# Reordering the start of an attention-plus-FFN kernel: loads, turns and sums of the first attention, pacing of batch 1, place of the late weight pieces

## The chip, the cores and the metric

One core of a Trainium2 chip. The metric is the device time of one execution in microseconds (us). Most executions of a program agree within a few tenths of a per cent; here they scatter by about 1%. The engines are called PE (TensorE, matmuls), DVE (VectorE), ACT (ScalarE), POOL (GpSimd) and SP (SyncE, which only issues DMAs here).

## The reference

```python
# q, k, v: (8 batches, 12 heads, 448 tokens, 64), float32
scores = scale * q @ k^T
m = max(scores); e = exp(scores - m)
attn = e / (sum(e) + exp(-m) + 1e-9) @ v           # softmax with one more term in the sum
x = attn, heads side by side                       # (3584 tokens, 768)
xn = x / sqrt(mean(x*x) + 1e-6) * rms_g
out = (silu(xn @ w_gate) * (xn @ w_val)) @ w_out    # 768 -> 1536 -> 768
```

## The kernel before

The program is one long PE stream. Batch 0's attention runs first ("first attention"). Then the FFN runs batch by batch and, between its matmul groups, the attention of the batches after it. A table of `(nominal time, operation)` says where each piece of attention work goes into the FFN's stream; the nominal times only fix an order. The matmul groups used as landmarks below are "gate m" and "value m", six matmuls each, for column block m of `w_gate` and `w_val`.

Heads go in pairs, and pairs in groups of two, three groups to a batch. For groups 0 to 6, PE transposes q and k ("turns" them, `emit_T`). From group 7 on a DMA does that (`turn_qk`, issued by SP), after POOL has cast q and k to bf16:

```python
    def cast_qkv(n, i, eng):
        ...
        eng.tensor_copy(out=dst, in_=staged[n, i].rearrange("p h c d -> p c h d"))

    def turn_qk(n):
        for i, src in enumerate((qk_bf[n, 0], qk_bf[n, 1])):
            nc.sync.dma_start_transpose(
                out=turned(n)[:, i, 0:LQ].rearrange("p (b t) -> p b t", t=P),
                in_=src.rearrange("p c h d -> p (c h d)"))
```

POOL issues the early loads too, and it works in program order. This is the part of batch 1's table that decides POOL's order (NG is 3, so `2 * NG + 1` is group 7 and `2 * NG + 2` is group 8):

```python
    for t, f in ((2.4, lambda: cast_qkv(NG, 2, G)), (3.5, lambda: loads(NG + 2)),
                 (3.6, lambda: cast_qkv(NG + 1, 2, G)), (3.7, lambda: load_w(4)),
                 (7.3, lambda: loads(2 * NG)), (7.4, lambda: cast_qkv(NG + 2, 2, G)),
                 (10.5, lambda: loads(2 * NG + 1)), (19.5, lambda: cast_qkv(2 * NG, 2, G)),
                 (19.6, lambda: casts(2 * NG + 1)), (19.7, lambda: loads(2 * NG + 2)),
                 (23.0, lambda: turn_qk(2 * NG + 1)), (26.0, lambda: casts(2 * NG + 2)),
                 (29.0, lambda: turn_qk(2 * NG + 2))):
        ops.append((t, f))
    for i in range(KF // 4):
        ops.append((22.0 + 0.01 * i, lambda i=i: load_w_o(i)))      # w_out, 3 x 768 KB
```

`warm(n)` issues n matmuls on zeros whose results nobody reads; they keep PE busy where it would idle:

```python
    def warm(n):
        ps = ps_f.tile([128, 512], FP32, name="warm_ps", tag="f")
        for _ in range(n):
            nc.tensor.matmul(ps, lhsT=blank[:, 0:128], rhs=blank, start=True, stop=True)
```

The softmax here doesn't subtract the row's maximum and nothing guards it: scores larger than these inputs give would overflow.

## Time and profile before

| | before |
|---|---|
| median of 3 runs | 485.04 us (484.3 to 485.96) |
| span of the profiled execution | 483.3 us |
| first FFN matmul | 39.4 us |
| PE busy | 95% of the span |

From the page of the kernel before, the busy time by engine, and then two rows of the 40 slices (12 us each). A digit is the busy share in tenths, and PEclk is the granted TensorE clock in tenths of full speed:

```profile
PE 460.6 (95%) x4053; PEld 247.9 (51%) x4056; DVE 242.0 (50%) x625; ACT 250.6 (52%) x363; POOL 98.4 (20%) x119
...
PE   8978988899989999999999999999999999999996
...
PEclk9999899999999999999999999999999999999998
```

PE fills nearly everything after the eighth slice. What is open lies in the first 90 us, and there PEclk has one dip, at about 50 us.

The window table of the kernel before: a stretch, its length, each engine's busy time, the mean granted clock, the DMA engines' share and GB/s.

```profile
36.00:48.00 12.00, 9.91 (x92) 5.08 (x93) 7.26 (x15) 6.12 (x9) 3.21 (x5) 1.00 0.16 41
48.00:60.00 12.00, 10.47 (x123) 5.49 (x123) 5.33 (x12) 8.55 (x12) 6.93 (x10) 0.86 1.16 213
60.00:76.00 16.00, 13.79 (x195) 7.99 (x192) 10.97 (x32) 11.88 (x16) 2.50 (x4) 1.00 0.95 191
76.00:88.00 12.00, 9.29 (x96) 5.26 (x96) 11.51 (x30) 3.92 (x9) 5.54 (x6) 1.00 0.07 13
88.00:105.00 17.00, 16.90 (x142) 8.48 (x138) 8.80 (x20) 10.00 (x14) 9.68 (x12) 1.00 1.05 236
105.00:120.00 15.00, 15.00 (x138) 7.75 (x138) 7.62 (x18) 9.39 (x13) 1.04 (x1) 1.00 1.21 180
```

PE has holes up to 88 us and none after. A clock of 0.86 in 48 to 60 us is 3.4 us at half speed.

The timeline of ACT in the kernel before, the first attention (start, duration, instruction, and in brackets the idle time before it and who ended it):

```profile
18.80 3.53 ACT L210 ACTIVATE p_sb_108<-s_ps 112x896 bf16<-112x896 f32 x4 [0.74 <-PE s_ps L205]
...
27.09 1.82 ACT L210 ACTIVATE p_sb_114<-s_ps 112x896 bf16<-112x896 f32 x2 [1.07 <-PE s_ps L205]
```

ACT, which has the most to do there, stands idle for scores that wait for a turn. That is what the first part of the change is aimed at.

### The profile page before, as it was taken

To read this page: it belongs to the slowest core of one execution; us is meant where nothing else is said; L and a number is where in the kernel's file an instruction comes from. 1 tells how busy PE (TensorE), PEld (TensorE's weight loads), DVE (VectorE), ACT (ScalarE), POOL (GpSimd) and SP (SyncE) were. 2 spreads that over 40 slices of the span, in tenths; PEclk is the share of its full clock that TensorE was granted. 3 is DMA by queue.
4 is the path that set the end of the run, shared out by engine and by line. 5 is a ranking of instruction groups with operands and counts; after the bars stand their busy time and mean duration, and the time that the engine had idled before them with its cause. 6 is when DMAs were issued, how large, how long until landed. Compare 5 with 4: busy or idle time off the path is not lost.

```text
span 483.3 us, 9859 instructions
## 1 busy us (share of the span) xinstructions
PE 460.6 (95%) x4053; PEld 247.9 (51%) x4056; DVE 242.0 (50%) x625; ACT 250.6 (52%) x363; POOL 98.4 (20%) x119
## 2 busy tenths in 40 slices
PE   8978988899989999999999999999999999999996
PEld 3544444455545555455455555554455555555563
DVE  4585469655634145855643136665653147655200
ACT  4975774555555665454556555554555562222221
POOL 6432511740403022313003012304001001000000
PEclk9999899999999999999999999999999999999998
DMA  8991990799919989289009979279104320200133
GB/s 121 205 222 35 217 229 16 182 227 181 219 40 230 182 207 200 62 198 182 1 20 229 182 181 212 51 151 210 27 2 114 96 80 3 55 1 1 34 98 99
DMA packets 86841, 60.48 MB, mean 125 GB/s; under 512 B 50710, under 2 KB 81756, under 8 KB 86796
## 3 DMA queue, kind: packets, MB, share of 16 engines
q1 hardware_dynamic: 73820, 43.60, 42.2%
q0 software_dynamic: 12976, 16.26, 18.0%
q8 instruction: 32, 0.52, 0.4%
q14 instruction: 13, 0.11, 0.1%
HBM read 47.19 MB, written 11.01 MB: 120 GB/s over the span
## 4 chain that ended last, share of the span: by engine, by line
PE 80%; issue 8%; DVE 6%; POOL 3%; ACT 2%; POOLq 0%; DVEq 0%
PE o_ps L335 23%; PE v_ps L310 19%; PE g_ps L310 15%; PE u_ps L235 8%; PE s_ps L205 8%; PE s_ps L310 5%; DVE xsq L261 2%; PE warm_ps L354 2%; DVE x_sb L239 1%; DVE ht_sb L321 1%; POOL v_sb_120 L154 1%; ACT t_sb L314 1%; PE qkt_ps L178 1%; ACT wg_bf L119 1%; DVE pair_t_102 L181 0%
## 5 line engine op out<-in xcount | busy, mean ns | idle before, releaser
L310 PE MATMUL v_ps<-xnt_sb,wv_bf 128*128 128x448 bf16 x576 | 126.3, 355 | 3.4 <-DVE ht_sb L321 3.1
L335 PE MATMUL o_ps<-wo_bf,ht_sb 128*128 128x384 bf16 x672 | 116.5, 326 | 0.0
L310 PE MATMUL g_ps<-xnt_sb,wg_bf 128*128 128x448 bf16 x444 | 96.3, 353 | 1.1 <-DVE xnt_sb L280 0.7
L335 PEld LDWEIGHTS <-ht_sb 128*128 128x128 bf16 x672 | 62.6, 98 | 46.2 <-issue 7.8
L310 PEld LDWEIGHTS <-wv_bf 128*128 128x128 bf16 x576 | 53.0, 98 | 56.2 <-issue 12.3
L310 PEld LDWEIGHTS <-wg_bf 128*128 128x128 bf16 x576 | 52.5, 98 | 54.5 <-issue 11.2
L314 ACT ACTIVATE t_sb<-g_ps 128x448 f32<-128x448 f32 x74 | 40.2, 543 | 73.3 <-PE g_ps L310 73.1
L210 ACT ACTIVATE p_sb_108<-s_ps 112x896 bf16<-112x896 f32 x64 | 55.8, 915 | 17.1 <-PE s_ps L205 17.1
L210 ACT ACTIVATE p_sb_114<-s_ps 112x896 bf16<-112x896 f32 x64 | 56.3, 915 | 12.5 <-PE s_ps L205 12.5
L338 ACT ACTIVATE out_sb<-o_ps 128x384 f32<-128x384 f32 x56 | 27.4, 490 | 66.9 <-PE o_ps L335 61.9
L210 ACT ACTIVATE p_sb_111<-s_ps 112x896 bf16<-112x896 f32 x64 | 55.8, 916 | 11.0 <-PE s_ps L205 11.0
L238 DVE RECIPROCAL recip<-u_ps 112x4 f32<-112x4 f32 x96 | 17.0, 177 | 81.9 <-PE u_ps L235 81.8
L293 POOL TENSOR_TENSOR rinv<-ms,neghalf 112x2 f32<-112x2 f32 x16 | 11.1, 716 | 157.3 <-DVE ms L286 149.6
L239 DVE TENSOR_TENSOR x_sb<-u_ps,recip 112x256 bf16<-112x256 f32 x96 | 40.7, 424 | 3.3
L154 POOL CAST q_bf<-q_f 112x1024 bf16<-112x1024 f32 x17 | 18.0, 1059 | 103.4 <-DMA q_f<-in_q_dram 90.1
L205 PE MATMUL s_ps<-qk_t 64*128 64x448 bf16 x272 | 37.5, 354 | 0.0
L261 DVE CUSTOM_DVE_ANT_0 xsq<-x_sb 112x256 bf16<-112x256 bf16 (+3 forms) x64 | 36.0, 563 | 1.7
L314 ACT ACTIVATE t_sb<-s_ps 128x448 f32<-128x448 f32 x22 | 11.9, 543 | 38.5 <-PE s_ps L310 33.3
L310 PE MATMUL s_ps<-xnt_sb,wg_bf 128*128 128x448 bf16 x132 | 28.6, 352 | 0.0
L235 PEld LDWEIGHTS <-p_sb_114 112*128 112x128 bf16 (+1 forms) x512 | 20.0, 98 | 7.7 <-DVE x_sb L239 1.4
L235 PEld LDWEIGHTS <-p_sb_108 112*128 112x128 bf16 (+1 forms) x512 | 19.8, 99 | 7.2 <-issue 2.9
L235 PEld LDWEIGHTS <-p_sb_111 112*128 112x128 bf16 (+1 forms) x512 | 19.7, 97 | 6.7 <-issue 2.1
(274 smaller groups left out, 385.6 us busy)
## 6 DMA issues: line engine op xcount, KB each, us to landing
q_f<-in_q_dram SPq DMA_DIRECT2D x15, 448.0 KB, 4.9
k_f<-in_k_dram SPq DMA_DIRECT2D x15, 448.0 KB, 6.2
v_f<-in_v_dram SPq DMA_DIRECT2D x15, 448.0 KB, 6.9
v_f<-in_v_dram POOLq DMA_DIRECT2D x9, 448.0 KB, 10.5
out_dram<-out_sb SPq DMA_DIRECT2D x8, 336.0 KB, 2.8
wg_bf<-in_moe_w_gate_dram POOLq DMA_DIRECT2D x4, 576.0 KB, 8.1
wv_bf<-in_moe_w_val_dram POOLq DMA_DIRECT2D x4, 576.0 KB, 12.5
wo_bf<-in_moe_w_out_dram POOLq DMA_DIRECT2D x3, 768.0 KB, 20.7
```

The source lines that it names most:

```text
L154: eng.tensor_copy(out=dst, in_=staged[n, i].rearrange("p h c d -> p c h d"))
L205: nc.tensor.matmul(s_ps[:, hh, 0:S], lhsT=k_t[r, k0:k0 + 128], rhs=qs[r], start=True, stop=True)
L210: nc.scalar.activation(out=p_v, in_=s_ps[0:P, :, 0:S], func=AF.Exp, scale=scale)
L235: nc.tensor.matmul(u_ps[:, qc, :], lhsT=p_sb[0:K, q0:q0 + 128], rhs=v_sb[0:K, c, h, :], start=(c == 0), stop=(c == C - 1))
L238: nc.vector.reciprocal(out=recip, in_=u_ps[0:P, :, D:E1])
L239: nc.vector.tensor_tensor(out=x_tiles[b][:, :, h * D:(h + 1) * D], in0=u_ps[0:P, :, 0:D], in1=recip.to_broadcast([P, C, D]), op=ALU.mult)
L261: nc.vector.tensor_tensor_reduce(out=xsq[:, 0:n], in0=x_c, in1=x_c, scale=1.0, scalar=0.0, op0=ALU.mult, op1=ALU.add, accum_out=acc)
L293: nc.gpsimd.tensor_tensor(out=rinv[:, cs], in0=ms[:, cs], in1=neghalf[:, cs], op=ALU.pow)
L310: nc.tensor.matmul(ps[:, 0:S], lhsT=w[:, dk, m * 128:(m + 1) * 128], rhs=xnt_tiles[b][:, :, dk, :], start=(dk == 0), stop=(dk == KD - 1))
L314: nc.scalar.activation(out=t, in_=ps[:, 0:S], func=AF.Tanh, scale=0.5)
L335: nc.tensor.matmul(o_ps[:, 0:HN], lhsT=ht_tiles[b2][:, fk, c * 128:(c + 1) * 128], rhs=wo_bf[:, fk, n * HN:(n + 1) * HN], start=(fk == 0), ...
L338: nc.scalar.activation(out=o_sb[:, n * HN:(n + 1) * HN], in_=o_ps[:, 0:HN], func=AF.Copy, scale=0.5)
```

## The change

The intent: let each pair's weighted sums run one pair behind its scores, place the turns where q and k arrive, move v casts off VectorE, and issue the late pieces of the gate and value weights among the loads of batch 1 so that the DMA engines don't idle from 36 to 46 us. The core of the diff:

```diff
-            if part == len(parts(b)) - 1 and b < NPE and c % 2 == 1:
+            if part > 0 and b < NPE and c % 2 == 1:              # more sums of squares on ACT
...
-        for cs in (slice(0, 2), slice(2, 4)):
-            nc.gpsimd.tensor_tensor(out=rinv[:, cs], in0=ms[:, cs], in1=neghalf[:, cs], op=ALU.pow)
+        nc.gpsimd.tensor_tensor(out=rinv, in0=ms, in1=neghalf, op=ALU.pow)
...
-    for j, t0 in enumerate((4.0, 5.6, 7.2, 8.8, 10.4, 12.0)):
-        ops += [(t0 + 0.39 * i, op) for i, op in enumerate(micro_ops(NP + j))]
+    for j, t0 in enumerate((3.6, 5.6, 7.6, 9.6, 11.6, 13.6)):
+        ops += [(t0 + 0.49 * i, op) for i, op in enumerate(micro_ops(NP + j))]
...
-    for i in range(2 * KD):
-        ops.append((9.0 + 0.45 * i, lambda: scale_w(1, V)))
+    for i in range(KD):
+        ops.append((9.6 + 0.35 * i, lambda: scale_w(1, V)))
+    ops.append((14.65, lambda: scale_w(KD, V)))
...
-    for t, f in ((2.4, lambda: cast_qkv(NG, 2, G)), (3.5, lambda: loads(NG + 2)),
-                 (3.6, lambda: cast_qkv(NG + 1, 2, G)), (3.7, lambda: load_w(4)),
-                 (7.3, lambda: loads(2 * NG)), (7.4, lambda: cast_qkv(NG + 2, 2, G)),
-                 (10.5, lambda: loads(2 * NG + 1)), (19.5, lambda: cast_qkv(2 * NG, 2, G)),
-                 (19.6, lambda: casts(2 * NG + 1)), (19.7, lambda: loads(2 * NG + 2)),
-                 (23.0, lambda: turn_qk(2 * NG + 1)), (26.0, lambda: casts(2 * NG + 2)),
-                 (29.0, lambda: turn_qk(2 * NG + 2))):
+    for t, f in ((2.4, lambda: (cast_qkv(NG, 2, G), load_w(2))),
+                 (4.3, lambda: (loads(NG + 2), cast_qkv(NG + 1, 2, G), load_w(2))),
+                 (8.3, lambda: loads(2 * NG)),
+                 (11.5, lambda: (cast_qkv(NG + 2, 2, G), loads(2 * NG + 1))),
+                 (17.1, lambda: (cast_qkv(2 * NG, 2, G), loads(2 * NG + 2))),
+                 (23.0, lambda: casts(2 * NG + 1)), (25.0, lambda: turn_qk(2 * NG + 1)),
+                 (27.5, lambda: casts(2 * NG + 2)), (29.5, lambda: turn_qk(2 * NG + 2))):
         ops.append((t, f))
     for i in range(KF // 4):
-        ops.append((22.0 + 0.01 * i, lambda i=i: load_w_o(i)))
+        ops.append((20.0 + 0.01 * i, lambda i=i: load_w_o(i)))
...
-    for i in range(2):
-        load_qkv(1, i, G)
     load_qkv(0, 2, G)
     make_identity(nc, ident_f)
+    loads(1)
...
-        (2, 1): [lambda: emit_AV(0, 0)], (2, 2): [lambda: emit_AV(0, 1)],
+        (1, 1): [lambda: emit_AV(0, 0)], (1, 2): [lambda: emit_AV(0, 1)],
+        (1, 3): [lambda: emit_T(2), lambda: load_w(4), lambda: cast_qkv(1, 2, G)],
... (the rest of this table moves in the same way)
```

More of the change, by code (lines that the diff above doesn't have):

```diff
@@ L430 @@
         ffn += [(TB, lambda b2=b2, c=c, n=n: emit_B(b2, c, n)) for c in range(7) for n in range(2)]
-    spans = {2: (20, 55), 3: (55, 88), 4: (88, 134), 5: (134, 171), 6: (171, 213), 7: (213, 250)}
+    spans = {2: (21, 55), 3: (55, 88), 4: (88, 134), 5: (134, 171), 6: (171, 213), 7: (213, 250)}
     ops = []
@@ L437 @@
         ops += [(t0 + (t1 - t0) * i / len(seq), op) for i, op in enumerate(seq)]
-    for j, t0 in enumerate((2.3, 3.4, 5.6, 7.2, 8.8, 10.4, 18.6, 22.0)):
+    for j, t0 in enumerate((2.3, 4.2, 6.2, 8.2, 11.2, 12.2, 19.5, 22.5)):
         ops.append((t0, lambda j=j: emit_T(NP + j)))
-    for j, t0 in enumerate((4.0, 5.6, 7.2, 8.8, 10.4, 12.0)):
-        ops += [(t0 + 0.39 * i, op) for i, op in enumerate(micro_ops(NP + j))]
-    ops.append((14.9, lambda: (emit_stats(1, 1), emit_root(1))))
+    for j, t0 in enumerate((3.6, 5.6, 7.6, 9.6, 11.6, 13.6)):
+        ops += [(t0 + 0.49 * i, op) for i, op in enumerate(micro_ops(NP + j))]
+    ops.append((16.7, lambda: (emit_stats(1, 1), emit_root(1))))
     for c in range(C):
-        ops.append((16.5 + 0.6 * c, lambda c=c: emit_scale(1, c)))
-        ops.append((18.7 + 1.1 * c, lambda c=c: emit_turn_x(1, c)))
-    for i in range(2 * KD):
-        ops.append((9.0 + 0.45 * i, lambda: scale_w(1, V)))
+        ops.append((18.3 + 0.6 * c, lambda c=c: emit_scale(1, c)))
+        ops.append((20.4 + 1.1 * c, lambda c=c: emit_turn_x(1, c)))
+    for i in range(KD):
+        ops.append((9.6 + 0.35 * i, lambda: scale_w(1, V)))
+    ops.append((14.65, lambda: scale_w(KD, V)))
     def loads(n):
@@ L494 @@
     between = {
-        (0, 0): [lambda: emit_T(1), lambda: [load_qkv(2, i, G) for i in range(2)]],
-        (0, 1): [gains, lambda: warm(1)], (0, 2): [lambda: warm(2)], (0, 3): [lambda: warm(2)],
-        (1, 0): [lambda: warm(2)], (1, 1): [lambda: warm(2)],
-        (1, 2): [lambda: emit_T(2), lambda: cast_qkv(0, 2, V)],
-        (1, 3): [lambda: [load_qkv(1, 2, G), load_qkv(2, 2, G), load_w(4)], lambda: warm(2)],
-        (2, 0): [lambda: warm(2)],
-        (2, 1): [lambda: emit_AV(0, 0)], (2, 2): [lambda: emit_AV(0, 1)],
@@ L502 @@
-        (2, 3): [lambda: emit_T(3), lambda: loads(NG)],
-        (3, 0): [lambda: emit_AV(1, 0)], (3, 1): [lambda: emit_AV(1, 1)],
-        (3, 2): [lambda: emit_T(4), lambda: cast_qkv(1, 2, V)],
-        (3, 3): [lambda: warm(2)],
-        (4, 0): [lambda: emit_AV(2, 0), lambda: cast_qkv(2, 2, V)],
-        (4, 1): [lambda: emit_AV(2, 1), lambda: emit_stats(0, 0, (0, 1))],
-        (4, 2): [lambda: emit_T(5), lambda: emit_stats(0, 0, (2, 3)), lambda: loads(NG + 1)],
-        (4, 3): [lambda: emit_AV(3, 0)],
@@ L510 @@
-        (5, 0): [lambda: emit_AV(3, 1)], (5, 1): [lambda: emit_AV(4, 0)],
-        (5, 2): [lambda: emit_AV(4, 1), lambda: emit_stats(0, 1, (0, 1))],
-        (5, 3): [lambda: emit_stats(0, 1, (2, 3))],
+        (0, 0): [lambda: emit_T(1)],
+        (0, 1): [gains, lambda: [load_qkv(2, i, G) for i in range(2)], lambda: warm(1)],
+        (0, 2): [lambda: cast_qkv(0, 2, V), lambda: load_qkv(2, 2, G), lambda: warm(2)],
+        (0, 3): [lambda: warm(2)],
+        (1, 0): [lambda: warm(2)],
+        (1, 1): [lambda: emit_AV(0, 0)], (1, 2): [lambda: emit_AV(0, 1)],
@@ new lines @@
+        (1, 3): [lambda: emit_T(2), lambda: load_w(4), lambda: cast_qkv(1, 2, G)],
+        (2, 0): [lambda: emit_T(3)],
+        (2, 1): [lambda: emit_AV(1, 0)], (2, 2): [lambda: emit_AV(1, 1)],
+        (2, 3): [lambda: loads(NG), lambda: warm(1)],
+        (3, 0): [lambda: warm(1), lambda: cast_qkv(2, 2, G)],
+        (3, 1): [lambda: emit_AV(2, 0)], (3, 2): [lambda: emit_AV(2, 1)],
+        (3, 3): [lambda: emit_T(4), lambda: emit_stats(0, 0, (0, 1))],
+        (4, 0): [lambda: emit_T(5), lambda: emit_stats(0, 0, (2,))],
@@ L513 @@
+        (4, 1): [lambda: emit_AV(3, 0), lambda: emit_stats(0, 0, (3,))],
+        (4, 2): [lambda: emit_AV(3, 1), lambda: loads(NG + 1)],
+        (4, 3): [lambda: warm(1)],
+        (5, 0): [lambda: warm(1)],
+        (5, 1): [lambda: emit_AV(4, 0)], (5, 2): [lambda: emit_AV(4, 1)],
+        (5, 3): [lambda: emit_stats(0, 1)],
     }
@@ L518 @@
                 f()
-    scale_w(3, A)
     emit_AV(NP - 1, 0)
     emit_AV(NP - 1, 1)
+    scale_w(1, A)
     emit_root(0)
-    scale_w(3, V)
+    scale_w(2, V)
+    scale_w(1, A)
     warm(14)
@@ L526 @@
         emit_scale(0, c)
+    scale_w(1, V)
     for c in range(C):
         emit_turn_x(0, c)
+    scale_w(1, V)
     scale_w(3, A)
```

## The prediction

> **What bounds the kernel now.** The page gives TensorE (PE) 95% busy over 483.3 us and 80% of the chain that ended last. By the window table PE is busy 387 of 395 us from 88 us on, which the change hardly touches. What can be won lies before:
>
> 1. First attention, 7.9 to 31.2 us: 24 exponentials on ACT, busy 20.8 of 23.3 us. The timeline shows it idle 0.74 us at 18.8, 0.23 at 23.4, 1.07 at 27.1, 0.41 at 29.3, waiting for scores, which wait for VectorE's copy of turned q/k, behind v casts (0.69 us) and sums of squares (0.56).
> 2. Norm, scale and turn of batch 0, 31.2 to 39.4 us: VectorE first has 4 sums of 0.43 us; the root is two POOL operations (0.91, 0.68).
> 3. First FFN with batch 1's attention, 39.4 to 88 us: PE idles about 7 us. Scores wait for exponentials 3.8 us in seven waits; u waits 1.31 us for VectorE at 78.5; scores wait 1.15 us at 87.9 for a copy queued behind x scales. The granted clock is halved for 3.4 us at 51, costing about 1.7 us; this fits the Trainium skill, "TensorE: Matmul & The Clock Gate", "What's actually happening" (half rate after an idle window of about 3.4 us).
>
> DMA is full from 8 to 36 us, then idle to 46 us: POOL waits 8.8 us for a q buffer before issuing the late weight pieces, which land at 56 to 65 us.
>
> **What the change does.**
> - Sums one pair behind, v loaded earlier, turns spread, two v casts moved to POOL (1.06 us each, off the path): two of six turns still stand directly before their scores, so about 1.4 of 2.45 us ACT idle stays. Gain 1.0 us.
> - Two of four second-part sums go to ACT, one root operation for two: VectorE frees 0.95 us, partly given back by 0.37 us of weight scaling between x scales and turns. Gain 0.4 us.
> - Late weights come before the q loads, landing at 41 to 56 us. Batch 1's pairs are spaced 2.0 units, not 1.6, so ACT has more FFN time per pair: 3.8 us of waits fall to 1.5, gain 2.3 us. The half-clock window may vanish (even chance): 0.9 us.
> - POOL's q and k casts leave batch 1's x scales. Two scales under casts took 2.08 us instead of 0.84, as "SBUF — State Buffer", "Who interferes with whom" has it (an exclusive port pair). The 1.15 us wait mostly goes: gain 0.8 us.
> - Against it: six late value-weight scalings (0.37 us each) now stand in one lump before the matmuls that use them, behind 1.4 us of sums: PE waits 1.5 to 2.5 us, net loss 0.8 us. Four fewer warm matmuls: nothing.
>
> Sum 4.6 us; some waits reappear elsewhere, so about 4.2 us.
>
> **Predicted time 480.8 us, range 477.6 to 484.2.** Faster by over 2%: 0.02; within 2%: 0.96; slower by over 2%: 0.02.
>
> **What would show it.** Right: batch 0's last exponential ends near 30 us; first FFN matmul near 38.0; scores' waits on exponentials from 40 to 80 us under 2 us; late weights landed by 57 us; a PE wait of over 1 us on wv_bf or VectorE around 76; everything after 88 us the same, 4 us earlier. Wrong: first FFN matmul still at 39.4, or a longer part after 88.
>
> **What would make it wrong.** v first delays the second q/k group past its turn and stalls ACT; the lump of scalings stalls PE over 3 us; the half-clock window returns or comes twice, as fewer warm matmuls and a new wait fall together; wo and batch-2 loads delay the turns so that scores wait near 105 us.

(The page that it names in quotation marks is of the Trainium skill. The half-clock window at 51 us: PE's two waits before that window were 1.14 and 0.44 us.)

## The result

| | before | after |
|---|---|---|
| median, same rounds | 485.5 us (484.3 to 486.48, 4 runs) | 492.94 us (492.06 to 494.6, 4 runs) |
| span of the profile | 483.3 us | 491.2 us |
| first FFN matmul | 39.4 us | 40.7 us |

The ratio is 1.0158, 95% interval 1.0122 to 1.0195. A ratio here is the mean time of one kernel's fast runs over that of the other's of the same rounds, so it is not quite the ratio of the medians quoted. A second set of runs of the same kernel, told below, gave 1.0124 (1.0084 to 1.0163). The predicted 480.8 us, and the range up to 484.2, were wrong: the change lost 5 to 7.5 us (by the medians of the two sets) where it was to gain 4.

The page of the changed kernel, the same two rows and the chain that ended last by engine:

```profile
PE   7887798969999999999999999999999999999996
...
PEclk9999998997999999999999999999999999999999
...
PE 81%; DVE 7%; ACT 5%; DMA 3%; POOL 2%; issue 1%; DVEq 0%; ACTq 0%
```

PEclk now dips in the seventh and, deeper, in the tenth slice, that is about 79 us and 110 us. A DMA has entered the chain with 3%, which is some 15 us. The kernel before had none there.

The window table of the changed kernel, same stretches:

```profile
36.00:48.00 12.00, 8.79 (x87) 4.49 (x84) 7.84 (x16) 5.47 (x8) 3.37 (x4) 1.00 0.66 113
48.00:60.00 12.00, 9.33 (x105) 4.93 (x102) 4.25 (x10) 8.81 (x12) 4.64 (x6) 1.00 0.98 175
60.00:76.00 16.00, 14.80 (x209) 8.23 (x206) 12.14 (x34) 11.47 (x15) 5.73 (x7) 1.00 0.66 147
76.00:88.00 12.00, 9.65 (x80) 5.16 (x79) 8.79 (x27) 3.80 (x9) 1.53 (x2) 0.86 0.00 0
88.00:105.00 17.00, 16.99 (x153) 8.84 (x152) 10.27 (x22) 10.07 (x15) 10.96 (x13) 1.00 0.98 199
105.00:120.00 15.00, 10.73 (x83) 5.19 (x82) 4.26 (x10) 4.46 (x7) 3.13 (x3) 0.77 1.17 212
```

From 105 to 120 us PE executed 83 matmuls where the kernel before executed 138. It was busy 10.7 us of 15, and at a mean clock of 0.77. The waits of PE from 88 to 120 us, first the kernel before:

```profile
PE s_ps L205 <- DVE pair_t_102 L181: 1.1, 1, 1.1
```

and the changed kernel (total us, times, longest):

```profile
PE s_ps L205 <- DMA qk_t<-k_bf: 4.3, 1, 4.3
```

The timeline of PE in the changed kernel around that wait:

```profile
111.00 0.93 PE L205 MATMUL s_ps<-qk_t 64*128 64x448 bf16 x4 [4.27 <-DMA qk_t<-k_bf]
111.86 2.42 PE L309 MATMUL v_ps<-xnt_sb,wv_bf 128*128 128x448 bf16 x6
```

Scores of the first pair of group 7 wait 4.27 us for the DMA that turns k. The six value matmuls after them take 2.42 us, where six take 1.3 us elsewhere: the clock was halved at 109.5 us, in the midst of the wait, and stayed so until 116.3.

Where the difference arises can be read from when the same matmul groups start. This table is worked out from the traces (start of a group's first weight load; us later than in the kernel before):

```
group                     before    after          after, second profile
batch 0, gate 0            39.38    40.71  +1.33    38.00  -1.38
batch 0, value 5           73.15    70.44  -2.71    69.86  -3.29
batch 0, gate 8            82.56    84.57  +2.01    84.17  +1.62
batch 0, gate 9            88.33    88.70  +0.37    88.31  -0.02
batch 1, gate 2           103.66   105.40  +1.74   105.01  +1.35
batch 1, value 4          111.53   120.10  +8.57   120.19  +8.65
batch 2, gate 0           174.75   181.94  +7.19   182.03  +7.28
```

Up to 104 us the changed kernel is not far from the old one. Between 105 and 120 us it falls 6.8 us behind (8.57 less 1.74). This is the wait of 4.27 us, plus some 2.65 us: half of the 5.3 us from 111.0 to 116.3, because work at half clock takes twice as long. Together 6.9 us.

Why did the turn land so late? The timeline of POOL, first the kernel before:

```profile
84.78 1.16 POOL L154 CAST q_bf<-q_f 112x1024 bf16<-112x1024 f32 x1
85.89 1.16 POOL L154 CAST k_bf<-k_f 112x1024 bf16<-112x1024 f32 x1
...
88.11 0.74 POOL L143 DMA_DIRECT2D q_f<-in_q_dram  x1
...
90.24 2.29 POOL L125 DMA_DIRECT2D wo_bf<-in_moe_w_out_dram  x3
```

and the changed kernel:

```profile
88.46 0.87 POOL L143 DMA_DIRECT2D q_f<-in_q_dram  x1
89.33 0.71 POOL L143 DMA_DIRECT2D k_f<-in_k_dram  x1
90.03 0.71 POOL L143 DMA_DIRECT2D v_f<-in_v_dram  x1
90.73 2.28 POOL L125 DMA_DIRECT2D wo_bf<-in_moe_w_out_dram  x3
92.98 1.08 POOL L154 CAST q_bf<-q_f 112x1024 bf16<-112x1024 f32 x1
93.96 1.08 POOL L154 CAST k_bf<-k_f 112x1024 bf16<-112x1024 f32 x1
```

In the kernel before the casts of group 7 come first and then the loads. In the changed kernel the loads of group 8 and of `w_out` come first: three of 448 KB and three of 768 KB, 3.6 MB. The turns of group 7 from issue to landing, before (the view of the tile `qk_t`, from 85 to 90 us):

```profile
L167 SPq DMA_TRANSPOSE qk_t<-k_bf x1: 1287/1287/1287, 87.3 to 87.3; - x1
...
DMA to landing us min/median/max: 3.1/3.2/3.3
```

and after (from 90 to 97 us):

```profile
L167 SPq DMA_TRANSPOSE qk_t<-k_bf x1: 6714/6714/6714, 95.5 to 95.5; - x1
...
DMA to landing us min/median/max: 13.9/14.6/15.4
```

The turn of k was issued 8 us later and then took 15.4 us instead of 3.1. Issuing it alone held SP for 6.7 us.

The records of the DMA packets show how the loads slowed the turns. First no packet of a turn moved for 3.9 us after the issue at 94.1 us (1.3 us in the kernel before). Then the two shared the DMA engines. This is the DMA view of the changed kernel from 99 to 107 us: queue, packets, MB, and share of the engines' time. In this stretch q0 carries POOL's loads and q1 the turns:

```profile
q0 software_dynamic: 920, 1.37, 93.8%
q1 hardware_dynamic: 921, 0.23, 21.9%
```

The packets alternate one to one, but a load's packet is 1536 bytes here and a turn's 256, so the turns got one seventh of the bytes. When this text says "queued behind loads", it means this sharing and not a strict order.

### The profile page after: what moved, and what is told of

Its sections match the earlier page's. It is cut to its first block, busy times and chain, and to the rows that moved or that the text cites. A ratio compares the mean times of both kernels' runs of the same rounds, so it can differ in the third digit from the quotient of the medians.

```text
span 491.2 us, 9841 instructions
## 1 busy us (share of the span) xinstructions
PE 464.8 (95%) x4048; PEld 249.7 (51%) x4052; DVE 240.3 (49%) x620; ACT 251.0 (51%) x366; POOL 98.2 (20%) x113
## 4 chain that ended last, share of the span: by engine, by line
PE 81%; DVE 7%; ACT 5%; DMA 3%; POOL 2%; issue 1%; DVEq 0%; ACTq 0%
PE o_ps L334 23%; PE v_ps L309 19%; PE g_ps L309 15%; PE u_ps L235 8%; PE s_ps L205 8%; PE s_ps L309 5%; DMA qk_t<-k_bf 3%; DVE xsq L261 2%; ACT p_sb_114 L210 1%; PE warm_ps L353 1%; ACT t_sb L313 1%; PE qkt_ps L178 1%; DVE x_sb L239 1%; ACT p_sb_111 L210 1%; DVE ht_sb L320 1%
## 5 line engine op out<-in xcount | busy, mean ns | idle before, releaser
L309 PE MATMUL g_ps<-xnt_sb,wg_bf 128*128 128x448 bf16 x444 | 97.7, 357 | 1.5 <-DVE xnt_sb L280 0.7
L309 PEld LDWEIGHTS <-wv_bf 128*128 128x128 bf16 x576 | 53.1, 98 | 58.4 <-issue 12.3
L309 PEld LDWEIGHTS <-wg_bf 128*128 128x128 bf16 x576 | 52.8, 98 | 55.7 <-issue 13.3
L210 ACT ACTIVATE p_sb_111<-s_ps 112x896 bf16<-112x896 f32 x64 | 56.3, 916 | 10.2 <-PE s_ps L205 10.0
L239 DVE TENSOR_TENSOR x_sb<-u_ps,recip 112x256 bf16<-112x256 f32 x96 | 40.7, 424 | 3.3
L292 POOL TENSOR_TENSOR rinv<-ms,neghalf 112x4 f32<-112x4 f32 x8 | 8.3, 1033 | 161.8 <-DVE ms L286 154.6
L261 DVE CUSTOM_DVE_ANT_0 xsq<-x_sb 112x256 bf16<-112x256 bf16 (+3 forms) x62 | 34.6, 559 | 1.6
```

The lines of the kernel that those rows point to most:

```text
L210: nc.scalar.activation(out=p_v, in_=s_ps[0:P, :, 0:S], func=AF.Exp, scale=scale)
L239: nc.vector.tensor_tensor(out=x_tiles[b][:, :, h * D:(h + 1) * D], in0=u_ps[0:P, :, 0:D], in1=recip.to_broadcast([P, C, D]), op=ALU.mult)
L261: nc.vector.tensor_tensor_reduce(out=xsq[:, 0:n], in0=x_c, in1=x_c, scale=1.0, scalar=0.0, op0=ALU.mult, op1=ALU.add, accum_out=acc)
L292: nc.gpsimd.tensor_tensor(out=rinv, in0=ms, in1=neghalf, op=ALU.pow)
L309: nc.tensor.matmul(ps[:, 0:S], lhsT=w[:, dk, m * 128:(m + 1) * 128], rhs=xnt_tiles[b][:, :, dk, :], start=(dk == 0), stop=(dk == KD - 1))
```

## The experiments

Theory Q: the loss is the turn of group 7, queued behind loads that POOL issued first, and the half clock that follows the wait. Rival H: it is the half clock at the start, the lump of six weight scalings, and the half clock at 79 us. Rival P: the late issue matters, not the bytes ahead. The first four runs were on one chip. There the kernel before had 486.78 us median (484.13 to 489.19, 11 runs).

### turn_early: the casts of group 7 before the loads again

```diff
-                 (17.1, lambda: (cast_qkv(2 * NG, 2, G), loads(2 * NG + 2))),
-                 (23.0, lambda: casts(2 * NG + 1)), (25.0, lambda: turn_qk(2 * NG + 1)),
+                 (17.1, lambda: (cast_qkv(2 * NG, 2, G), casts(2 * NG + 1), loads(2 * NG + 2))),
+                 (25.0, lambda: turn_qk(2 * NG + 1)),
```

> The changed kernel with one line changed: the three POOL casts of group 7 (the first group whose q and k are turned by DMA) stand before the POOL loads of group 8 and of wo, as in the kernel before; all else of the change stays. Theory Q (the turn is queued in the DMA engines behind about 3.7 MB of loads that POOL issued first, PE waits 4.3 us for it and then runs 5.3 us at half clock): the turn lands near 93 us, the wait near 111 us and the half-clock window after it vanish, 6 to 7.5 us are won, time 485 to 487 us, so the change without this is within 0.4% of the kernel before. Rival H (the loss lies in the longer half-clock start, the lump of weight scalings and the half-clock window at 79 us; the turn's wait only shows where they come to light): time stays above 489 us.

Measured: 486.78 us median (484.91 to 488.75, 6 runs), ratio to the kernel before 1.0009 (0.9965 to 1.0053). The view of `qk_t` from 85 to 92 us:

```profile
DMA to landing us min/median/max: 3.1/3.2/3.3
```

The k turn landed at 93.3 us. No DMA ended a wait of PE from 88 to 120 us, and the clock was 1.00 from 88 to 120 us. Theory Q holds; H, which wanted over 489, falls. The whole measurable loss goes with one line of order. What stays is that the rest of the change gains nothing either.

### before_tail: the new order alone, in the kernel before

```diff
-                 (19.6, lambda: casts(2 * NG + 1)), (19.7, lambda: loads(2 * NG + 2)),
-                 (23.0, lambda: turn_qk(2 * NG + 1)), ...
+                 (19.6, lambda: loads(2 * NG + 2)),
+                 (23.0, lambda: casts(2 * NG + 1)), (25.0, lambda: turn_qk(2 * NG + 1)), ...
```

(`w_out` stays at 22.0, which now is before the casts.)

> The kernel before with only this order taken from the change: the loads of group 8 and of wo are issued before the casts of group 7. Theory Q: the turn of group 7 is issued near 93 us, lands after 105 us, PE waits 2 to 6 us for it and loses 1 to 3 us more at half clock; time 489 to 494 us. Rival H: within 1 us of the kernel before.

Measured: 494.67 us median (492.62 to 496.37, 6 runs), ratio 1.0169 (1.0129 to 1.021); the median is 0.7 us above what was expected. Its waits of PE from 88 to 120 us:

```profile
PE s_ps L205 <- DMA qk_t<-k_bf: 7.5, 1, 7.5
```

The wait was longer than the 2 to 6 us expected, and again the clock was halved just then, from 111.3 to 118.1 us. But this edit moved more than POOL's order. The turn went from 23.0 to 25.0 in the table, and in the kernel before that lets SP issue three loads of its own (448 KB each) ahead of it:

```profile
92.40 0.35 SPq L143 DMA_DIRECT2D q_f<-in_q_dram  x1
...
94.72 11.95 SPq L167 DMA_TRANSPOSE qk_t<-q_bf  x1
106.71 4.63 SPq L167 DMA_TRANSPOSE qk_t<-k_bf  x1
```

So the new order on POOL and SP together suffices to cause the loss. That POOL's order causes it by itself is shown by turn_early, where SP's order stayed as it was.

### wo_late: only the loads of `w_out` behind the casts

```diff
-        ops.append((20.0 + 0.01 * i, lambda i=i: load_w_o(i)))
+        ops.append((26.0 + 0.01 * i, lambda i=i: load_w_o(i)))
```

> The changed kernel with the loads of wo issued after the casts of group 7, not before; the casts still stand after the loads of group 8. Theory Q: the turn is issued near 92 us with 1.3 MB ahead of it and not 3.7 MB, lands by 100 us, no wait near 107 us; time 485 to 487.5 us. Rival P (it is the late issue of the turn by 8 us, from POOL's order, that matters, not the bytes ahead): the issue moves by only 2.3 us, so at least 1.5 us of wait and some half clock stay, time 488 to 491 us.

Measured: 489.87 us median (488.73 to 491.81, 6 runs), ratio 1.0072 (1.0032 to 1.0111). By the time alone P would seem right. The profile says otherwise. The turns were issued at 90.8 and 92.2 us, only some 3 us earlier than in the changed kernel, and yet the view of `qk_t` from 90 to 94 us has

```profile
DMA to landing us min/median/max: 6.5/8.2/9.9
```

so the k turn landed at 102.1 us, 2 us later than Q expected, and no wait for it is left. P falls: the issue moved by some 3 us and the landing by 8.9. The turn took 15.4 us with all 3.6 MB of loads issued ahead of it, 9.9 with group 8's 1.3 MB, and 3.1 with none. The bytes ahead are not the whole account, though: group 8's last load had landed at 96.4 us, and the k turn needed 5.7 us more, beside the loads of `w_out` that POOL issued from 92.8 us, just after it. The time was lost to something new. DVE's timeline in this run:

```profile
89.03 4.07 DVE L266 TENSOR_SCALAR x_sb<-x_sb,rinv 112x768 bf16<-112x768 bf16 x2
```

Two scalings of x, which take 0.42 us each alone, took 4.07 us beside the three POOL casts that now run from 89.7 to 92.9 us. PE waited 1.84 us for DVE behind them, and a half-clock window from 94.1 to 97.5 us came on top. Q's account holds in that the wait is gone; the time expected from it was exceeded by 2.4 us, and I had not asked what the casts would collide with. That the collision cost these 2.4 us is read from this one profile; no run tests it.

### first_only: the new first attention with the old batch 1

The part of the changed kernel up to the first FFN matmul, and the table of batch 1 of the kernel before.

> The first attention of the change (order of loads, sums, turns, v casts, sums of squares, one root) with batch 1's schedule of the kernel before. If the start at half clock that lasted to 13.9 us in the changed kernel's profile is chance and not caused by the change, this profile may show either 6.4 or 13.9 us; with 6.4 us the first FFN matmul comes near 38.7 us and the time is 0 to 1.5 us below the kernel before; with 13.9 us near 40.7 and 0 to 1.5 us above.

Measured: 485.96 us median (484.31 to 486.5, 6 runs), ratio 0.9982 (0.9946 to 1.0019): not distinguishable from the kernel before. The profile is neither of the two cases expected: full clock from 5.4 us, half clock once more from 8.9 to 12.3, first FFN matmul at 39.46 us. The run before_tail, which has the old first attention, had the same second half-clock window (8.9 to 12.3 us) and its first FFN matmul at 40.92. The window at the start therefore belongs to no kernel in particular. The difference of 1.46 us (40.92 against 39.46) is not the gain of the new first attention, since before_tail was at half clock once more, from 32.8 to 36.2 us, and first_only was not; a fairer pair comes with after_again below.

### lump_spread, casts_idle, both, first_idle

These four went together, to see whether the rest of the change can be made to pay. The kernel before had 485.55 us there (482.69 to 489.31, 11 runs).

lump_spread is turn_early with the late weight scalings spread out again:

```diff
-    for i in range(KD):
-        ops.append((9.6 + 0.35 * i, lambda: scale_w(1, V)))
-    ops.append((14.65, lambda: scale_w(KD, V)))
+    for i in range(2 * KD):
+        ops.append((9.0 + 0.45 * i, lambda: scale_w(1, V)))
```

> turn_early with the twelve late weight scalings of VectorE spread out again as in the kernel before (no lump of six before the value matmuls of the seventh column block). Theory L: the lump's wait of 1.2 us on wv_bf and the half-clock window that begins at 77 to 79 us in all three profiles with the lump (cost about 1.7 us) go; at the seventh to eighth column block 2 us or more are won against turn_early, time 2 to 3 us below turn_early's, about 484 us. Rival: VectorE's work only moves, PE waits about as long for another result of VectorE there (1.3 us on x_sb as in the kernel before), and a half-clock window falls elsewhere; time within 1 us of turn_early.

Measured: 484.84 us median (483.39 to 486.45), ratio 0.9986 (0.9948 to 1.0024). The 1.2 us wait for the value weights and the half-clock window at 77 to 79 us are gone; this profile had one at 52.8 us instead. The five profiles with the lump (after, after_again, turn_early, wo_late, casts_idle) all have a half-clock window that begins at 77 to 79 us, and none of the nine others does. Theory L holds for the profile. Of the 2 to 3 us expected in time the ratios, 0.9986 against 1.0009, show about 1.1, with overlapping intervals.

casts_idle is turn_early with the casts of group 7, and the last of group 6, in POOL's idle time:

```diff
-                 (17.1, lambda: (cast_qkv(2 * NG, 2, G), casts(2 * NG + 1), loads(2 * NG + 2))),
-                 (25.0, lambda: turn_qk(2 * NG + 1)),
+                 (12.6, lambda: (cast_qkv(2 * NG, 2, G), casts(2 * NG + 1), turn_qk(2 * NG + 1))),
+                 (17.1, lambda: loads(2 * NG + 2)),
```

> turn_early with the casts of group 7 and the last v cast of group 6 put into POOL's idle time before batch 1's root (data landed by 74 us), so that they no longer run beside VectorE's scaling of batch 1's x. Theory S (POOL casts and VectorE's scalings of x hold each other up): the four scalings take 0.4 to 0.5 us each instead of 0.7 to 1.2, the 0.65 us wait of scores near 90 us goes; the turn lands before 80 us; 0.7 to 1.5 us won against turn_early. Rival: the scalings take as long as before, or nothing is won because the wait for ht_sb at 86 us sets the pace; within 0.5 us.

Measured: 486.4 us median (485.47 to 487.66), ratio 1.0022 (0.9986 to 1.0058). The profile does what theory S says. The scalings of x from 80 to 95 us, durations in ns (min/median/max), in turn_early:

```profile
L266 DVE TENSOR_SCALAR x_sb<-x_sb,rinv x4: 402/1150/1193, 86.6 to 90.9; 112x768 bf16<-112x768 bf16 x4
```

and in casts_idle:

```profile
L266 DVE TENSOR_SCALAR x_sb<-x_sb,rinv x4: 401/438/524, 86.7 to 88.9; 112x768 bf16<-112x768 bf16 x4
```

The turns landed by 76.7 us. The time shows no gain: its mean granted clock over six runs was 0.987, against 0.989 in turn_early, and the lump stayed.

both puts the two edits together.

> lump_spread and casts_idle together. If L and S both hold, 3 to 4.5 us below turn_early and as much below the kernel before: about 482.5 to 484 us. If neither, within 1 us of both.

Measured: 483.26 us median (481.73 to 484.0), ratio 0.9954 (0.9919 to 0.999). This is the first version that is faster than the kernel before, by 2.3 us between the medians, less than the 3 to 4.5 us expected.

first_idle is first_only with the casts in idle time (same edit, at nominal 11.0).

> The first attention of the change with batch 1's schedule of the kernel before (first_only) and the casts of group 7 and the last of group 6 in POOL's idle time. Theory S: the x scalings that took 2.08 us for two under casts take 0.84, the wait of 1.1 to 1.7 us of scores near 88 us goes; 1 to 2 us below first_only, so 2 to 3 us below the kernel before. Rival: within 0.5 us of first_only.

Measured: 486.0 us median (484.67 to 486.66), ratio 1.0011 (0.9972 to 1.005). The scalings of x did fall (median 418 ns). But POOL's "idle" time was not free: beside the casts DVE's sums of squares (0.69 us alone) took up to 1.40 us, and PE waited 3.08 us for DVE at 79.6 us, where first_only has 1.31. The expectation of 1 to 2 us was missed.

### both_warm, both_again, after_again

Seven of the eight experiments' profiles so far have a half-clock window that begins between 36.7 and 39.7 us (the expectation below says five, a miscount). It comes after PE's waits around batch 0's x turns. both_warm adds twelve matmuls on zeros there and at the start (2, 5, 2 and 3; the expectations say ten, another miscount):

```diff
     warm(10)
     emit_T(0)
+    warm(2)
...
-    warm(14)
+    warm(19)
     for c in range(C):
         emit_scale(0, c)
     scale_w(1, V)
     for c in range(C):
         emit_turn_x(0, c)
+        if c % 2 == 1:
+            warm(2 + c // 2)
```

> The kernel of run both with ten more matmuls on zeros where PE waits in the first 40 us: two after the first turn, five more before batch 0's x turns, five in their gaps. Theory C (PE's idle time before the first FFN matmul, 1.3 + 0.5 + 0.7 us in a few us, brings the half-clock window at 37 to 45 us that five of eight earlier profiles show there): no half-clock window between 35 and 46 us, mean granted clock at least 0.994, 1 to 3 us below both_again of the same call. Rival: the windows come as often, or the added matmuls delay the work behind them by what they save; within 0.7 us of both_again.

> The kernel of run both, once more, on this call's chip: 0.3 to 0.7% below the kernel before.

> The changed kernel, once more, on this call's chip: 1.3 to 1.9% above the kernel before. Theory Q: this profile too shows a wait of 3 to 6 us of scores for the DMA turn near 107 us and a half-clock window after it. The length of the half-clock start and the windows before 90 us are free to differ from the first profile.

On this chip the kernel before had 486.76 us (483.69 to 489.49, 11 runs).

| | median us | ratio to before | mean granted clock of 6 runs |
|---|---|---|---|
| both_warm | 480.96 (480.03 to 481.7) | 0.9895 (0.9852 to 0.9937) | 0.998 |
| both_again | 482.67 (480.21 to 483.66) | 0.9922 (0.9881 to 0.9964) | 0.993 |
| after_again | 492.1 (491.71 to 493.05) | 1.0124 (1.0084 to 1.0163) | 0.983 |

The window table of both_warm, where the changed kernel had 0.86 and 0.77:

```profile
36.00:48.00 12.00, 10.11 (x85) 4.68 (x85) 6.95 (x15) 6.80 (x10) 4.34 (x6) 1.00 0.77 123
...
76.00:88.00 12.00, 11.23 (x128) 6.62 (x126) 9.54 (x27) 5.10 (x11) 6.60 (x8) 1.00 0.69 178
...
105.00:120.00 15.00, 15.00 (x138) 7.77 (x135) 7.47 (x17) 9.35 (x13) 4.51 (x5) 1.00 1.06 219
```

Twelve matmuls that compute nothing are worth about 1.5 us (difference of the means of six runs, 482.42 and 480.89), and both_warm is the fastest kernel. both_again was a little better than expected (0.78% against 0.3 to 0.7%). after_again's ratio lies just under the expected 1.3%, and its profile has the DMA wait, 4.92 us at 111.3 us.

after_again's profile also settles the first attention of the changed kernel. It had full clock from 7.0 us, and its first FFN matmul stands at 38.03 us, not at 40.74. The kernel before, at full clock from 6.4 us, has it at 39.41. Neither profile was at half clock between those starts and 37.7 us, so the new first attention is 1.38 us faster up to there:

```profile
38.03 2.40 PE L309 MATMUL g_ps<-xnt_sb,wg_bf 128*128 128x448 bf16 x6 [0.69 <-DVE xnt_sb L280]
```

Its last exponential of batch 0 ended at 29.7 us. In the first profile of the same kernel the clock was half until 13.9 us. The line also shows what followed in this execution: six matmuls in 2.40 us, at half clock.

### before_warm: the twelve matmuls in the kernel before

The same three edits, nothing else.

> The kernel before with the same ten extra matmuls on zeros and nothing else. Theory C: the half-clock windows before 46 us and the one near 51 us become rare, mean granted clock rises from about 0.989 to at least 0.994, time 2 to 3.5 us below the kernel before. Rival (the matmuls pay only in run both, because its idle time lies otherwise): within 1 us of the kernel before.

Measured: 484.3 us median (482.74 to 485.55, 6 runs), against 485.02 for the kernel before (one of its 11 executions, at 535.85 us and a clock of 0.847, is left out of the ratio); ratio 0.9981 (0.9946 to 1.0017). Its mean granted clock was 0.997, and the profile has no half-clock window between 6 and 480 us. The clock rose as theory C says; the expected 2 to 3.5 us did not come. On this call the kernel before had a mean clock of 0.992 in its fast runs, so less was to be had. How much the matmuls are worth there stays open.

## Why the prediction was wrong

- **The step that failed**: "everything after 88 us the same, 4 us earlier". The change put the loads of group 8 and `w_out` ahead of the casts of group 7 in POOL's order. The DMA turn then took 15.4 us instead of 3.1, PE waited 4.27 us, and the clock was halved for 6.8 us about that wait, which cost some 2.65 us more: 6.9 us lost between 105 and 120 us. turn_early takes this back; before_tail, which moves SP's loads too, makes it appear in the kernel before. The prediction named it as the last item of what could make it wrong and gave it no weight. The trace of before already showed the danger: the turn of group 8, issued at 94.7 us behind `w_out`, took 21.0 us to land. It was not needed until later. The Trainium skill, "DMA: Bandwidth & Descriptors", "Issuing engines are not separate DMA queues", says that DMAs of all issuing engines run on the same 16 DMA engines; this case agrees, with SP's turns delayed from 3.2 to 14.6 us (medians) by loads that POOL issued.
- **First attention and root** (gain 1.0 and 0.4): right. First FFN matmul predicted at 38.0 us; 38.03 in the second profile, 1.38 us before the kernel before at like clock. The first profile's 40.74 was the longer start at half clock. In time it is not shown: first_only is at 0.9982 with an interval that holds 1.
- **Batch 1's pacing** (waits on exponentials 3.8 us falling to 1.5): wrong. In 40 to 80 us the changed kernel's scores wait 4.1 us for ACT (2.0, 1.4 and 0.6 by buffer). Between gate 0 and value 5 of batch 0 it gains 4.0 us on the old kernel, since less attention work stands there (244 matmuls, not 284). It gives 4.7 us back by gate 8, where that work, the lump and a half-clock window come due.
- **Late weights landed by 57 us**: the gate pieces came at 43.2 and 46.0 us, the value pieces at 58.3 and 61.2, because POOL still waited 8.8 us for a q buffer between them. PE did not wait for a load of them.
- **The lump**: expected 1.5 to 2.5 us of wait; it was 1.21 us, plus a half-clock window in each of five profiles (lump_spread has neither).
- **Scalings of x** (gain 0.8): the 1.15 us wait at 87.9 us went, but PE waited 0.91 us for another result of DVE at 87.0. That POOL and DVE hold each other up, as "SBUF — State Buffer", "Who interferes with whom" says, is shown by wo_late and casts_idle.
- **Half clock** ("may vanish, even chance"): wrong in direction. The six executions of after_again had a granted clock of 0.983 each. The 43 fast executions of the kernel before in these runs had 0.991 on average, from 0.980 to 1.000, and times from 482.69 to 489.49 us that go with the clock (correlation -0.94). The straight line through these 43 gives 0.34 us for each 0.001. By this estimate the half clock costs the changed kernel some 6 us an execution and the kernel before some 3. It is rough: the recorded clock leaves out the slow start and counts the last few microseconds, when PE is done.

Left open: why the rest of the change (turn_early) shows no gain in time though its first FFN matmul comes 1.05 us earlier. Its profile ran 10.2 us at half clock between 30 and 90 us and that of the kernel before 3.4 us. The lump accounts for 3.4 us of the difference. No run has the pacing of batch 1 by itself, so its own worth is not known.

## What to carry to other kernels

When loads are moved forward, look at what stands behind them in every queue of the DMA engines: a small transfer with a deadline should be issued before megabytes without one, whichever engine issues it, and early enough to land before they get going (the k turn of wo_late, issued 0.6 us before `w_out`'s loads, still took 9.9 us). On an engine that issues DMAs in program order and computes as well, the place of a cast decides when a transfer on another queue starts and what computation it collides with, so check both sides of the move. A wait of a few microseconds on PE should be costed with the half clock it can bring, here 2.65 us on top of 4.27; and a comparison of less than 1% needs the granted clock of each execution beside its time.

## What the Trainium skill lacked or had wrong

- "DMA: Bandwidth & Descriptors", "SWDGE vs HWDGE vs iDMA", states that software and hardware DMAs feed different queues of a DMA engine, "and the engine round-robins between them". The changed kernel agrees, with 920 packets of loads and 921 of turns from 99 to 107 us. What is lacking is what follows for a transpose: at 256 bytes a packet against 1536 it got a seventh of the bytes, and the k turns of after, after_again and before_tail landed at 110.95, 111.21 and 113.46 us, each 0.7 to 2.0 us after the last `w_out` load that was issued ahead of it (110.22, 110.46, 111.43). No section gives the latency of a DMA transpose behind queued loads: 3.1 us with none ahead, 9.9 with 1.3 MB, 15.4 with 3.6 MB.
- The same page does not say that issuing a transpose can hold SP: 6.71 us in the changed kernel against 1.29 in the kernel before (k turn of group 7), and 16.04 in wo_late (q turn of group 8).
- "TensorE: Matmul & The Clock Gate", "HAM oscillation — how this bites in real kernels", gives as the abstract rule no idle gaps of PE over about 3.4 us; a later section tells of frequent short idles, without a figure. Here short gaps went before half clock too: 0.35, 0.44 and 1.21 us within 75.1 to 77.8 us were followed by half clock from 78.8 to 82.2 us. In all 14 profiles every half-clock window begins a whole number of steps of 3.413 us after the first clock record. Of the steps at full clock in which PE's idle time came to 1.55 us or more in sum, 24 of 26 were followed by half clock; from 1.30 to 1.55 us 4 of 15, and below that 1 of 813. This is a count from the matmul records, some of which can be missing, and not a tested rule. Its remark in "What's actually happening" that a ramp costs under 1% and varies from run to run agrees: the start at half clock ended at 7.0 us in one profile of the changed kernel and at 13.9 in the other, with the first FFN matmul 2.7 of 491 us later.
- "SBUF — State Buffer", "Who interferes with whom" is right that such operations block each other; a number for a DVE scaling under three casts is missing from it: 4.07 us for two that take 0.84 alone.
